# Local attention on quarter-array matmuls: 64 rows per head, unpadded keys, new priorities

## Chip, cores and metric

The kernel runs on one core of a Trainium2 chip. The metric is the device time of one execution in microseconds (us). The kernel before took 943.61 us (median of 3 runs, 941.19 to 946.57).

## What is computed

Attention of two kinds over 4 batches, 8 heads, 576 positions and 64 channels, their sum, and then two pairs of dense layers on the 2304 tokens:

```python
out_up = np.repeat(sm_attn(q_d, k_d, v_d), factor, axis=2)   # on means of 4 positions
mask = np.abs(pos[:, None] - pos[None, :]) < factor
scores = np.where(mask, scale * np.matmul(q, k.transpose(0, 1, 3, 2)), -1000000000.0)
...
out_local = np.matmul(attn, v)
x = (out_up + out_local)            # to [2304, 512]
h = x @ w_in;  y = (h * np.cos(h)) @ w_out          # first pair of layers
h = y @ w_in2; out = (np.maximum(h, 0.0) ** 2) @ w_out2   # second pair
```

## The kernel before

**Local attention** is done in units, `unit_l(b, d)`: 4 batches times 5 stretches of up to 116 queries, 20 units in all. A unit holds two blocks (`t`) of 58 queries, each against the 64 keys that can lie in its band, for 8 heads, which are held as 4 pairs (`pr`): 128 partitions hold the 64 channels of the even head of a pair and, below, those of the odd one. `f_s` makes the scores. The query tile of a pair and a block is the stationary operand (128 rows, 58 columns). The keys move, from a tile `kz` that has two copies of the columns: in one the odd head's rows are zero, in the other the even head's. So one matmul of 128 columns makes the scores of both heads, and the zeros keep them apart. Block 0 writes partitions 0 to 57 of the result, block 1 partitions 64 to 121. All 8 matmuls of a unit go into one bank of PSUM, on top of a bf16 matmul (L573) that puts the mask there. `softmax` runs on DVE and ACT, `f_t` transposes the weights on PE, `f_e` copies them on ACT into `pz`, which is zero-padded in the same way (two copies, one ACT instruction for each half of the partitions), and `f_pv` multiplies by the values, 8 matmuls again. `f_x` adds the up-sampled global part and writes the tokens to `xr`. The zeros of `kz` and `pz` are set once by POOL. `kz` and `pz` are two fixed tiles each, taken in turn; `q` and `v` have two buffers.

**Global attention** is 16 units `unit_g`. **The first pair of layers** runs in 5 rounds of 512 or 256 tokens (`mlp_h`, `mlp_o`, 16 blocks `f` each), in matmuls of fp32r; each number is split in a high and a low part, so each product is three matmuls (`mm3`, L666 to L668). Its weights are converted from float64 words on DVE (`convert`) as they arrive. A round can begin when its tokens are in `xr`. Of the 20 local units 5 come before the first round; the other 15 are put between the matmuls of rounds. **The second pair** (`big_h`, `big_o`) follows, from about 544 us on, with no attention in it.

**PSUM.** Four banks (`ps`) are shared by scores, transposes and results of the attention and by `mlp_h`; four more (`acc`) hold the sums of `mlp_o`.

**The order** on every engine is set before the run: the class `Plan` places the operations one by one, with costs and due times (`key`) that `OFF` shifts by operation and stage. Where the plan sees PE idle before the first `mlp_o`, it puts in small matmuls on zeros (`busy`, L1174), below called fills. Each engine works through its list in that order and waits on semaphores; SP issues the loads and stores in the same way. `IN_TURN` names the tiles whose buffers are given out in the order of the due times.

```python
nc.tensor.matmul(
    ps[64 * t:64 * t + QT, pr], T[q][:, t, pr, :], kz[kt][:, :, t, pr, :], start=False,
    stop=(pr == PR - 1),
)
```

Of the kernel before, what the change touches and what calls it, by code (L numbers as in the profile page):

```python
# [18 lines left out]
PR = H // 2  # L19
# [3 lines left out]
QT = 58  # L23
# [12 lines left out]
ADD_PE = 0  # L36
# [19 lines left out]
class Plan:  # L56


    RATE = {"SP": 1.24, "POOL": 2.07}
    LAT = {"PE": 0.15, "ACT": 0.15, "DVE": 0.15, "SP": 0.0, "POOL": 0.0}  # L60

    IN_TURN = ("rawi", "rawo", "w2", "p", "pt", "q", "v", "t", "w1")
# [45 lines left out]
    def order(self):  # L108
# [23 lines left out]
        stream = [x for o in sorted(ops, key=lambda o: o[2]) for x in o[5] if x[1] == "ws"]  # L132

        def room(inst, more=0):
            tag = inst[0]
            held = got[tag]
            at = len(held) + more
            if tag in self.IN_TURN and turn[tag][at] != inst:
                return None
            if inst[1] == "ws" and stream[0] != inst:  # L140
                return None
            if at < self.bufs[tag]:
                return 0.0
            last = [end[i] for i in self.users[held[at - self.bufs[tag]]]]
# [80 lines left out]
def body(ctx: ExitStack, tc: tile.TileContext, qb, kw, vw, qp, kp, vp, wi, wo, masks, ident, out_t):  # L225
    nc = tc.nc
    NR = len(ROUNDS)
    BUFS = {
        "q": 2, "v": 2, "rawi": 2, "rawo": 2, "wm": 1, "wa": 2, "w2": 3, "p": 3, "pt": 2, "t": 2, "ki": 2,
        "mx": 4, "sm": 4, "gh": 3, "gl": 3, "e": 2, "acc": 1, "ps": 4, "w1": PAIRS,  # L230
    }
    ATT = ("q", "v", "p", "pt", "mx", "sm")
# [170 lines left out]
    def load_local(b, d, key):  # L403
        q, v, kt = ("q", b, d), ("v", b, d), (b * ND + d) % 2

        def lq():
            nc.sync.dma_start(out=new(q, [128, 2, PR, QT]), in_=qb[b, d])
# [13 lines left out]
    def softmax(u, key, ps, p, view, np_, g, n, scale, on_act):  # L421
# [8 lines left out]
        def small(t):  # L430
            return T[t][0:np_, 0:g]
# [885 lines left out]
```

## Time and profile before

| | before |
|---|---|
| median of the runs, us | 943.61 (941.19 to 946.57) |
| the profiled execution, us | 936.85 |
| its span, first to last instruction, us | 935.0 |
| PE busy, us | 912.2 (98%) |
| DVE busy, us | 624.6 (67%) |
| ACT busy, us | 421.2 (45%) |
| granted clock of TensorE | 0.998 |
| first matmul of the first round, us from the start | 66.07 |

The rows name an engine, a line of kernel.py, the operation and its tiles (result, then operands). PE is the matmuls, PEld their weight loads. An fp32 matmul is two records of the profile (L579: 320 records of 160 matmuls), each with a weight load of its own. The busy time of a group is the union of its records, so records that run side by side are counted once, while the mean of one record is its length from issue to end. Idle time is charged to what ended it.

### The profile page before, as it was taken

Reading aid. Unit: us, or ns where it says so; the run is one execution under the profiler, and the core shown is the slowest. Engines: PE = TensorE matmul, PEld = TensorE weight load, DVE = VectorE, ACT = ScalarE, POOL = GpSimd, SP = SyncE. Lnnn points to the kernel's source line nnn. Section 1 sums busy time; section 2 is a strip of 40 time slices with the busy share of each in tenths; the row PEclk is TensorE's granted clock in tenths of the full one; section 3 lists DMA queues with packets and bytes.
Section 4 is the critical chain, followed back from the end, with each engine's and each line's share of the span. In section 5 each row is a group of like instructions: output and inputs, shape, how many; then the busy total and the mean of one; then the engine's idle time right before and its main releaser. Section 6 shows DMA issues by size and latency. Waiting matters only on the chain.

```text
span 935.0 us, 15239 instructions
## 1 busy us (share of the span) xinstructions
PE 912.2 (98%) x5794; PEld 793.7 (85%) x5794; DVE 624.6 (67%) x1106; ACT 421.2 (45%) x865; POOL 36.7 (4%) x53
## 2 busy tenths in 40 slices
PE   9999999999999999999999989999999999999997
PEld 9787787789788877888888879999999898999996
DVE  6898789744754269867897667878955454635351
ACT  1866568767766376656665522213221111121111
POOL 3001200220030000000000000000000000000000
PEclk9999999999999999999999999999999999999999
DMA  9876956994892255776897796878776555766543
GB/s 286 272 215 191 251 181 224 287 249 154 257 194 80 71 171 163 258 257 219 290 324 234 247 337 219 291 242 266 243 257 199 183 180 178 212 226 183 168 158 113
DMA packets 82569, 204.10 MB, mean 218 GB/s; under 512 B 9281, under 2 KB 18241, under 8 KB 82497
## 3 DMA queue, kind: packets, MB, share of 16 engines
q1 hardware_dynamic: 77888, 191.33, 62.1%
q0 software_dynamic: 4608, 11.80, 6.6%
q8 instruction: 46, 0.75, 0.3%
q14 instruction: 27, 0.21, 0.1%
HBM read 162.20 MB, written 40.89 MB: 217 GB/s over the span
## 4 chain that ended last, share of the span: by engine, by line
PE 72%; DMA 2%; ACT 1%; DVE 1%; issue 0%; SPq 0%; ACTq 0%; DVEq 0%
PE acc L666 9%; PE acc L667 9%; PE acc L668 9%; PE pp L666 6%; PE pp L667 6%; PE pp L668 6%; PE ps L666 5%; PE ps L667 5%; PE ps L668 5%; PE acx L1094 2%; PE acx L1095 2%; PE acx L1093 2%; DMA w<-w_dram 1%; PE ps L579 1%; PE ps L616 1%; PE ps L520 0%
## 5 line engine op out<-in xcount | busy, mean ns | idle before, releaser
L666 PE MATMUL ps<-xh,w 128*128 128x512 f32 (+1 forms) x320 | 120.8, 377 | 2.5 <-DVE t L706 1.9
L666 PE MATMUL acc<-gh,w 128*128 128x512 f32 (+1 forms) x320 | 120.3, 376 | 0.7 <-DMA w<-w_dram 0.7
L668 PE MATMUL acc<-gh,w 128*128 128x512 f32 (+1 forms) x320 | 118.1, 369 | 1.0 <-DVE w L276 1.0
L667 PE MATMUL ps<-xl,w 128*128 128x512 f32 (+1 forms) x320 | 118.0, 369 | 0.5 <-DVE xl L276 0.5
L668 PE MATMUL ps<-xh,w 128*128 128x512 f32 (+1 forms) x320 | 117.8, 368 | 0.0
L667 PE MATMUL acc<-gl,w 128*128 128x512 f32 (+1 forms) x320 | 117.8, 368 | 0.0
L276 DVE TENSOR_TENSOR gl<-t,gh 128x512 fp32r<-128x512 f32 (+1 forms) x80 | 50.7, 635 | 46.4 <-ACT gh L273 45.6
L706 DVE TENSOR_TENSOR t<-t,ps 128x512 f32<-128x512 f32 (+1 forms) x80 | 50.5, 632 | 39.3 <-ACT t L703 39.1
L1066 DVE TENSOR_TENSOR xl<-c,xh 128x768 fp32r<-128x768 f32 x32 | 30.6, 956 | 68.4 <-ACT xh L1063 68.2
L666 PEld LDWEIGHTS ps<-xh,w 128*128 128x128 f32 x320 | 60.2, 188 | 16.4 <-DVE t L706 3.6
L668 PEld LDWEIGHTS acc<-gh,w 128*128 128x128 f32 x320 | 60.3, 188 | 12.0 <-DVE w L276 1.8
L666 PEld LDWEIGHTS acc<-gh,w 128*128 128x128 f32 x320 | 60.3, 188 | 11.9 <-issue 1.4
L1025 DVE TENSOR_TENSOR c<-ua,pp 128x384 f32<-128x384 f32 x96 | 52.8, 552 | 24.9 <-PE pp L668 21.4
L667 PEld LDWEIGHTS ps<-xl,w 128*128 128x128 f32 x320 | 60.3, 188 | 10.2 <-DVE xl L276 0.9
L1063 ACT ACTIVATE xh<-c 128x768 fp32r<-128x768 f32 x32 | 27.0, 845 | 93.0 <-PE acc L668 84.6
L668 PEld LDWEIGHTS ps<-xh,w 128*128 128x128 f32 x320 | 60.3, 188 | 10.1
L667 PEld LDWEIGHTS acc<-gl,w 128*128 128x128 f32 x320 | 60.4, 189 | 9.4
L711 ACT ACTIVATE t<-t 128x512 f32<-128x512 f32 (+1 forms) x80 | 46.7, 585 | 47.9 <-DVE t L698 46.9
L694 ACT ACTIVATE ki<-ps 128x512 int32<-128x512 f32 (+1 forms) x80 | 43.6, 550 | 43.5 <-PE ps L668 35.8
L273 ACT ACTIVATE gh<-t 128x512 fp32r<-128x512 f32 (+1 forms) x80 | 46.6, 583 | 32.1 <-PE acc L668 27.5
L698 DVE SCALAR_TENSOR_TENSOR t<-ki,ps 128x512 f32<-128x512 int32 (+1 forms) x80 | 50.0, 629 | 7.7 <-ACT ki L694 6.9
L703 ACT ACTIVATE t<-t,halfpi 128x512 f32<-128x512 f32 (+1 forms) x80 | 54.1, 678 | 1.8
(163 smaller groups left out, 2103.2 us busy)
## 6 DMA issues: line engine op xcount, KB each, us to landing
w<-w_dram SPq DMA_DIRECT2D x96, 512.0 KB, 3.7
gl<-w_dram SPq DMA_DIRECT2D x84, 256.0 KB, 3.2
gh<-w_dram SPq DMA_DIRECT2D x84, 256.0 KB, 3.7
rawi<-in_wi_dram SPq DMA_DIRECT2D x32, 512.0 KB, 6.0
rawo<-in_wo_dram SPq DMA_DIRECT2D x32, 512.0 KB, 5.7
w_dram<-w SPq DMA_DIRECT2D x32, 512.0 KB, 4.9
w_dram<-rawo SPq DMA_DIRECT2D x24, 512.0 KB, 4.2
v<-in_vw_dram SPq DMA_DIRECT2D x20, 256.0 KB, 4.2
```

The costliest lines, as they stand in the source:

```text
L273: nc.scalar.activation(out=hi(), in_=src(), func=AF.Copy)
L276: nc.vector.tensor_tensor(out=lo(), in0=src(), in1=hi().bitcast(F32), op=OP.subtract)
L666: nc.tensor.matmul(ps, w_hi, r_hi, start=first, stop=False)
L667: nc.tensor.matmul(ps, w_hi, r_lo, start=False, stop=False)
L668: nc.tensor.matmul(ps, w_lo, r_hi, start=False, stop=last)
L694: nc.scalar.activation(out=tt(ki), in_=tt(hp), func=AF.Copy, scale=1.0 / TWO_PI)
L698: nc.vector.scalar_tensor_tensor(out=tt(t), in0=tt(ki), scalar=-TWO_PI, in1=tt(hp), op0=OP.mult, op1=OP.add)
L703: nc.scalar.activation(out=tt(t), in_=tt(t), func=AF.Sin, scale=-1.0, bias=halfpi[:, 0:1])
L706: nc.vector.tensor_tensor(out=tt(t), in0=tt(t), in1=tt(hp), op=OP.mult)
L711: "ACT", act(n), key + 0.2, lambda: nc.scalar.activation(out=tt(t), in_=tt(t), func=AF.Abs), w=[t]
L1025: nc.vector.tensor_tensor(out=out(), in0=a(), in1=ps(), op=OP.subtract if sub else OP.add)
L1066: nc.vector.tensor_tensor(out=gpart(1, R, f), in0=T[t], in1=gpart(0, R, f).bitcast(F32), op=OP.subtract)
```

## The change

- `unit_l` has no padded tiles. Keys are a tile `k` of 128 partitions, loaded by one transfer in place of two; `pz` is a tile without the second copy.
- Each score matmul works on 64 rows (one head) and writes 58 partitions: 64 columns, 16 matmuls a unit in place of 8 of 128 columns. Even heads write one bank, odd heads another. Neighbours in the list use different row halves; two heads and two blocks make four quarters of the array. The mask is added twice, 256 columns each.
- The values' product goes the same way: 16 matmuls of 58 columns on 64 rows, in two banks, in place of 8 of 116 columns on 128 rows.
- `softmax` reads the scores from two banks: maximum and subtraction are two instructions each, on half the columns. `f_x` is two instructions per piece. `f_e` is one ACT instruction of 128 partitions in place of two of 64.
- `q`, `k` and `v` have three buffers, `pz` two. POOL's memsets go.
- The plan takes the turn of buffers from the order in which operations are written; all of `OFF` is new, so all engines' lists are in a new order.

```diff
-ADD_PE = 0
...
-OFF = {('SP|body.<lambda>|wid', 0): -8.1, ('SP|body.<lambda>|wmf', 0): -24.5,
+OFF = {('SP|body.<lambda>|wid', 0): -472.0, ('SP|body.<lambda>|wmf', 0): 129.9,
...
-        for i in sorted(range(n), key=lambda i: (ops[i][2], i)):
-            for inst in ops[i][5]:
+        for o in ops:
+            for inst in o[5]:
                 turn[inst[0]].append(inst)
-        stream = [x for o in sorted(ops, key=lambda o: o[2]) for x in o[5] if x[1] == "ws"]
+        stream = [x for o in ops for x in o[5] if x[1] == "ws"]
...
-        "q": 2, "v": 2, "rawi": 2, "rawo": 2, ...
+        "q": 3, "k": 3, "v": 3, "pz": 2, "rawi": 2, "rawo": 2, ...
...
-            nc.vector.tensor_reduce(out=small(mx), in_=view(), op=OP.max, axis=AX.X)
+            nc.vector.tensor_reduce(out=small(mx)[:, i::m], in_=views[i](), op=OP.max, axis=AX.X)
...
         def f_s():
-            ps = new(s, [128, PR, 2, KT], space=PSUM)
             new(p, [128, 512])
-            nc.tensor.matmul(
-                ps.rearrange("p r h n -> p (r h) n"), id16, mask16[:, mk:mk + 1, :].to_broadcast([128, 2 * PR, KT]),
-                start=True, stop=False,
-            )
+            for x in s:
+                nc.tensor.matmul(
+                    new(x, [128, PR, KT], space=PSUM), id16, mask16[:, mk:mk + 1, :].to_broadcast([128, PR, KT]),
+                    start=True, stop=False,
+                )
             for pr in range(PR):
                 for t in range(2):
-                    nc.tensor.matmul(
-                        ps[64 * t:64 * t + QT, pr], T[q][:, t, pr, :], kz[kt][:, :, t, pr, :], start=False,
-                        stop=(pr == PR - 1),
-                    )
+                    for h in range(2):
+                        nc.tensor.matmul(
+                            T[s[h]][64 * t:64 * t + QT, pr], T[q][half[h], t, pr, :], T[k][half[h], t, pr, :], start=False,
+                            stop=(pr == PR - 1),
+                        )
...
-        def f_e(hh):
-            pp = slice(64 * hh, 64 * hh + 64)
-            nc.scalar.activation(out=pz[kt][pp, :, :, hh, :], in_=T[tp][pp, :, :, 0:QT], func=AF.Copy)
+        def f_e():
+            nc.scalar.activation(out=T[pz], in_=T[tp][:, :, :, 0:QT], func=AF.Copy)
...
                 for j in range(2):
                     for par in range(2):
-                        nc.tensor.matmul(
-                            ps[64 * par:64 * par + 64, t, 2 * j:2 * j + 2, 0:m], T[v][:, t, 2 * j + par, :],
-                            pz[kt][:, 2 * j + par, t, :, 0:m], start=not on_pe, stop=j == 1 or not on_pe,
-                        )
+                        for h in range(2):
+                            nc.tensor.matmul(
+                                T[pv[h]][half[par], t, j, 0:m], T[v][half[h], t, 2 * j + par, :],
+                                T[pz][half[h], 2 * j + par, t, 0:m], start=True, stop=True,
+                            )
```

**PE between the first and the second round.** The list of PE where the last scores before the second round stand; `acc` rows are `mlp_o` of the first round, `x4` and `x8` are counts. Before:

```order
L592 MATMUL ps<-id_sb,p 128x128 x4
L666 MATMUL acc_1456<-gh,w_2142 128x512
L667 MATMUL acc_1456<-gl,w_2142 128x512
L668 MATMUL acc_1456<-gh,w_2142 128x512
L573 LDWEIGHTS id_68
L573 MATMUL ps<-mask_69,id_68 128x512
L579 MATMUL ps<-kz_70,q 58x128 x8
L616 MATMUL ps<-pz_72,v 64x116 x8
L573 LDWEIGHTS id_68
L573 MATMUL ps<-mask_69,id_68 128x512
L579 MATMUL ps<-kz_71,q 58x128 x8
L592 MATMUL ps<-id_sb,p 128x128 x4
```

After, the same place:

```order
L574 LDWEIGHTS id_68
L574 MATMUL ps<-mask_69,id_68 128x256
L574 LDWEIGHTS id_68
L574 MATMUL ps<-mask_69,id_68 128x256
L581 MATMUL ps<-k,q 58x64 x16
L574 LDWEIGHTS id_68
L574 MATMUL ps<-mask_69,id_68 128x256
L574 LDWEIGHTS id_68
L574 MATMUL ps<-mask_69,id_68 128x256
L581 MATMUL ps<-k,q 58x64 x16
L593 MATMUL ps<-id_sb,p 128x128 x4
L611 MATMUL ps<-pz,v 64x58 x32
```

The scores of two units now stand next to each other, and no matmul of the first round's layers stands between the attention's.

**SP at the start.** The list of loads from the first on; `up_sb` and `xr` take the parts of the pooled queries and keys, `rawi` and `rawo` the weights' words. Before:

```order
L414 DMA v<-in_vw_dram 128x512 x2
L291 DMA rawi<-in_wi_dram 128x1024 x2
L291 DMA rawo<-in_wo_dram 128x1024 x2
L1178 DMA mask_f<-in_masks_dram 128x192
L1176 DMA id_sb<-in_ident_dram 128x128
L407 DMA q<-in_qb_dram 128x464 x2
L358 DMA up_sb<-in_qp_dram 128x4x144 x4
L358 DMA xr<-in_kp_dram 128x4x144 x4
L411 DMA kz_70<-in_kw_dram 64x512
```

After:

```order
L288 DMA rawi<-in_wi_dram 128x1024 x2
L1164 DMA id_sb<-in_ident_dram 128x128
L355 DMA xr<-in_kp_dram 128x4x144 x4
L355 DMA up_sb<-in_qp_dram 128x4x144 x4
L288 DMA rawo<-in_wo_dram 128x1024
L288 DMA rawi<-in_wi_dram 128x1024
L288 DMA rawo<-in_wo_dram 128x1024
L406 DMA k<-in_kw_dram 128x512 x3
L406 DMA v<-in_vw_dram 128x512 x2
```

The pooled queries and keys moved ahead of the values, the mask, the local queries and the second matrix's weights. On PE the plan puts 180 small matmuls ahead of the first one of the attention, where 350 stood, and 645 in all ahead of the first round, where 646 stood.

**DVE in the units between the first and the second round.** `mx` is the maximum, L440 and L431 the subtraction, `sm` the sums. Before:

```order
L437 TENSOR_REDUCE mx<-ps 128x8
L440 TENSOR_TENSOR p<-ps,mx 128x512
L459 TENSOR_REDUCE sm<-p 128x8
L437 TENSOR_REDUCE mx<-ps 128x8
L463 TENSOR_SCALAR sm<-sm 128x8
```

After:

```order
L428 TENSOR_REDUCE mx<-ps 128x4 x2
L431 TENSOR_TENSOR p<-ps,mx 128x4x64 x2
L451 TENSOR_REDUCE sm<-p 128x8
L428 TENSOR_REDUCE mx<-ps 128x4
L455 TENSOR_SCALAR sm<-sm 128x8
```

The rows that read PSUM became two each, one for each bank.

## Rows read from the trace of the kernel before

**Rows 1.** The page: busy time, share of the span and instructions of each engine.

```profile
PE 912.2 (98%) x5794; PEld 793.7 (85%) x5794; DVE 624.6 (67%) x1106; ACT 421.2 (45%) x865; POOL 36.7 (4%) x53
```

**Rows 2.** Busy time by stretch: length; PE, PEld, DVE, ACT, POOL; clock, DMA share, GB/s.

```profile
0.00:20.00 20.00, 19.01 (x293) 19.01 (x294) 12.55 (x28) 3.81 (x5) 6.33 (x13) 1.00 0.93 283
...
40.00:140.00 100.00, 96.41 (x693) 79.45 (x692) 83.79 (x150) 65.53 (x151) 9.75 (x13) 1.00 0.72 211
140.00:300.00 160.00, 153.34 (x1179) 129.47 (x1178) 104.77 (x224) 115.27 (x283) 19.76 (x26) 1.00 0.77 211
300.00:440.00 140.00, 140.00 (x775) 113.00 (x774) 93.00 (x171) 82.91 (x151) 0.00 (x0) 1.00 0.53 181
440.00:560.00 120.00, 115.67 (x524) 96.09 (x523) 93.96 (x159) 66.44 (x113) 0.00 (x0) 1.00 0.82 286
```

**Rows 3.** Waits of PE and PEld: total us, times, longest.

```profile
PE ps L666 <- DVE t L706: 1.9, 4, 0.7
...
PEld ps L666 <- DVE t L706: 3.6, 8, 0.9
```

**Rows 4.** Group of the scores' matmuls: count, busy us, mean ns, idle before.

```profile
L579 PE MATMUL ps<-kz,q 128*58 128x128 f32 x320 | 21.8, 278 | 0.3 <-DMA kz<-in_kw_dram 0.2
```

**Rows 5.** Timeline of PE, a stretch of two units: start, length, count.

```profile
354.37 1.01 PE L616 MATMUL ps<-pz,v 128*64 128x116 f32 x16
355.32 0.39 PE L573 MATMUL ps<-mask,id 128*128 128x512 bf16 x1
355.64 1.09 PE L579 MATMUL ps<-kz,q 128*58 128x128 f32 x16
356.66 0.39 PE L573 MATMUL ps<-mask,id 128*128 128x512 bf16 x1
```

**Rows 6.** The same L579 group, records begun by 355.79, by 355.81, by 355.91.

```profile
355.64 0.32 PE L579 MATMUL ps<-kz,q 128*58 128x128 f32 x2
355.64 0.43 PE L579 MATMUL ps<-kz,q 128*58 128x128 f32 x4
355.64 0.54 PE L579 MATMUL ps<-kz,q 128*58 128x128 f32 x6
```

**Rows 7.** Timeline of PE before the first round (L1174 fills, L504 global scores).

```profile
0.99 22.36 PE L1174 MATMUL idle<-zero 128*128 128x128 bf16 x350 [0.99 <-DVE zero L1168]
24.13 1.88 PE L504 MATMUL ps<-kd_sb,qd_sb 128*96 128x144 f32 x12 [0.78 <-DVE kd_sb L368]
...
60.49 2.84 PE L1174 MATMUL idle<-zero 128*128 128x128 bf16 x48
...
66.07 0.48 PE L666 MATMUL ps<-xh,w 128*128 128x512 f32 x1
```

**Rows 8.** DVE before the first round: the first conversion, and mean ns by form.

```profile
8.23 0.43 DVE L295 TENSOR_SCALAR wm<-rawi 128x512 int32<-128x512 int32 x1 [6.08 <-DMA rawi<-in_wi_dram]
...
L302 DVE SCALAR_TENSOR_TENSOR wa<-rawi,wm 128x512 int32<-128x512 int32 x16 | 11.0, 690 | 0.4
...
L368 DVE TENSOR_TENSOR kd_sb<-kd_sb,xr 128x144 f32<-128x144 f32 x8 | 2.5, 308 | 0.3
```

**Rows 9.** Groups of the units' DVE and ACT work: count, busy us, mean ns.

```profile
L437 DVE TENSOR_REDUCE mx<-ps 128x8 f32<-128x512 f32 x20 | 13.7, 685 | 7.0 <-PE ps L579 6.9
...
L440 DVE TENSOR_TENSOR p<-ps,mx 128x512 f32<-128x512 f32 x16 | 10.8, 672 | 0.2
...
L642 DVE TENSOR_TENSOR xr<-ps,up_sb 128x464 f32<-128x464 f32 x13 | 8.2, 632 | 1.3 <-PE ps L616 1.3
...
L642 DVE TENSOR_TENSOR xr<-ps,up_sb 128x232 f32<-128x232 f32 x7 | 2.8, 395 | 1.2 <-PE ps L616 1.2
...
L596 ACT ACTIVATE pz<-ps 64x464 f32<-64x464 f32 x40 | 22.0, 551 | 7.3 <-PE ps L592 6.9
```

**Rows 10.** Busy time in one stretch between the first rounds (columns as rows 2).

```profile
175.00:180.00 5.00, 4.38 (x49) 3.40 (x45) 4.69 (x12) 3.50 (x9) 1.41 (x3) 1.00 1.03 347
```

**Rows 11.** L573 (the masks) from 300 to 440 us: count, durations, first and last start.

```profile
L573 PE MATMUL ps<-mask,id x5: 381/389/390, 344.5 to 356.7; 128*128 128x512 bf16 x5
```

More of the change, by code (lines that the diff above doesn't have):

```diff
@@ L475, in f_norm @@
             )
-        op("DVE", dve(g * n), key, f_max, r=[ps], w=[mx], new=[mx])
+        for i in range(m):
+            op(
+                "DVE", dve(g * n // m), key, lambda i=i: f_max(i), r=[ps[i]] + ([mx] if i else []), w=[("mx1",) + u] if i else [mx],
+                new=[] if i else [mx],
+            )
         if on_act:
-            op("ACT", g * act(n, 0.18) + 0.2, key + 0.02, f_exp_sum, r=[ps], w=[p, sm, mx], new=[sm], table="exp")
+            op("ACT", g * act(n, 0.18) + 0.2, key + 0.02, f_exp_sum, r=list(ps) + [("mx1",) + u] * (m - 1), w=[p, sm, mx], new=[sm], table="exp")
         else:
-            op("DVE", dve(g * n), key + 0.01, f_sub, r=[ps, mx], w=[p])
-            op("ACT", act(g * n), key + 0.02, f_exp, w=[p], table="exp")
+            for i in range(m):
+                op(
+                    "DVE", dve(g * n // m), key + 0.01, lambda i=i: f_sub(i), r=[ps[i], mx] + [("mx1",) + u] * (m - 1),
+                    w=[("p1",) + u] if i else [p],
+                )
+            op("ACT", act(g * n), key + 0.02, f_exp, r=[("p1",) + u] * (m - 1), w=[p], table="exp")
             op("DVE", dve(g * n), key + 0.03, f_sum, r=[p], w=[sm], new=[sm])
@@ L565, in unit_l @@
         u = ("l", b, d)
-        s, p, tp = ("ps", "s") + u, ("p",) + u, ("ps", "t") + u
-        q, v, kt = ("q", b, d), ("v", b, d), (b * ND + d) % 2
+        s, tp, pv = [("ps", "s", h) + u for h in range(2)], ("ps", "t") + u, [("ps", "pv", h) + u for h in range(2)]
+        p, q, k, v, pz = ("p",) + u, ("q", b, d), ("k", b, d), ("v", b, d), ("pz",) + u
         mk = {0: 0, ND - 1: 2}.get(d, 1)
+        half = [slice(0, 64), slice(64, 128)]
         def f_s():
-            ps = new(s, [128, PR, 2, KT], space=PSUM)
@@ L598, in unit_l @@
-        op("PE", 0.5, key + 0.1, f_t, r=[p, ("id",)], w=[tp], new=[tp])
-        for hh in range(2):
-            op("ACT", act(464), key + 0.1, lambda hh=hh: f_e(hh), r=[tp], w=[("pz", kt, hh)])
+        def f_e():
+            nc.scalar.activation(out=T[pz], in_=T[tp][:, :, :, 0:QT], func=AF.Copy)
+        op("PE", 0.6, key + 0.1, f_t, r=[p, ("id",)], w=[tp, pz], new=[tp, pz])
+        op("ACT", act(464), key + 0.1, f_e, r=[tp], w=[pz])
         s0 = DT * d
         n = min(DT, S - s0)
-        on_pe = b * ND + d < ADD_PE
@@ L604, in unit_l @@
-        pv = ("ps", "pv") + u
         def f_pv():
-            ps = new(pv, [128, 2, KD, QT], space=PSUM)
+            for x in pv:
+                new(x, [128, 2, 2, QT], space=PSUM)
             for t in range(2):
                 m = min(QT, n - t * QT)
-                if on_pe:
-                    nc.tensor.matmul(
-                        ps[:, t, :, 0:m], id_sb, up_sb[:, :, s0 + t * QT:s0 + t * QT + m], start=True, stop=False
-                    )
                 for j in range(2):
@@ L624, in unit_l @@
+        op(
+            "PE", 0.6, key + 0.2, f_pv, r=[v, pz] + [("up", c) for c in range(KD)], w=pv + xtok(b * S + s0, n), new=pv,
         )
```

93 lines of the change are left out of this document (36 added, 57 removed).

## Prediction, made before the changed kernel ran

> **What bounds the kernel now.** I read the page's busy times first. PE has work for 98% of the span, and DVE, the next, for 67% [rows 1]. Then the stretches: from 40 to 560 us PE stands idle for 3.6, 6.7, 0 and 4.3 us, about 14.6 us in all [rows 2]. So a microsecond that PE no longer needs between the rounds is worth up to a microsecond, unless another engine is right behind. The granted clock is full in every stretch [rows 2], so nothing is to be won or lost there unless PE falls idle for long. Third I looked at what PE waits for: the largest item between the rounds is the next block's scores bank, which L706 on DVE still reads, 1.9 and 3.6 us [rows 3]. The four `ps` banks are thus already a resource that PE waits for, though little. PE never waits for the units' keys for more than 0.3 us in all [rows 4], so third buffers have nothing to remove on PE. Last comes the time before the first round, which begins at 66.07 us [rows 7]. There the plan fills PE with matmuls on zeros, so a busy PE says nothing of the bound, and 350 fills alone take the first 23 us.
>
> **Part 1, the matmuls.** A unit's scores take from 355.64 to 356.66, 1.02 us, and its values' product from 354.37 to 355.32, 0.95 us [rows 5]. Each has 16 records. One record is listed at 278 ns [rows 4], so they overlap, and rows 6 show how: two records have begun by 355.79, four by 355.81, six by 355.91. They start in pairs, about 107 ns apart after the first step. That is what 2 x 128 columns take at 2.4 GHz (256 / 2.4 = 107 ns). So each record streams its columns twice, and the two blocks, which write different halves of the result's partitions, run side by side. The pairs could not form if a matmul's second record had to start ahead of the next matmul's first; records of different tiles pass each other. The scores are then 8 steps x 107 = 0.85 us and 0.17 us fixed (the first weights, the drain). The product is 8 x 2 x 116 / 2.4 = 0.77 us and 0.18 us fixed.
>
> Now there are 32 records of half the columns. If four run side by side (two blocks times two heads), it is 8 steps again, each 2 x 64 / 2.4 = 53 ns for the scores and 48 for the product. The first step of a group is 0.05 us longer than the others (355.64 to 355.80, against 0.107 us) [rows 6], which I take as the load of the first weights, so a step won't be shorter than about 55 ns. Scores 8 x 55 + 170 = 0.61 us (0.41 saved), product 8 x 55 + 180 = 0.62 us (0.33 saved). The mask is one matmul of 512 columns and 0.32 us from its start to the next one's [rows 5]; two of 256 have the same columns, 0.01 us more. **0.73 us a unit; 15 units between the rounds: -10.9 us.** No row shows 64-row halves side by side, so the bounds are wide. If the two halves don't overlap, it is 16 steps of 53 and 48 ns, 0.85 and 0.77 us: nothing saved. If not even the pairs formed, 32 steps would be 1.70 and 1.55 us, 1.6 us dearer a unit; the pairs in rows 6 speak against that. I take the first, since blocks already run side by side by the place they write to.
>
> One rule speaks against it. The rows show two records that begin less than 20 ns after each other and the next two some 100 ns later [rows 6]. The Trainium skill, "TensorE: Matmul & The Clock Gate", section "Wait — 56ns, not 53.3ns?", says that matmuls never start closer than about 25 ns, however few columns they have. By it four records would need an estimated 100 ns, as long as a pair does now, and the saving would be gone. The rows don't agree with it for neighbours in a pair.
>
> **Part 2, what it adds elsewhere.** DVE reads two banks: an addition of 464 columns takes 632 ns and one of 232 takes 395 [rows 9], so a split costs 2 x 395 - 632 = 0.16 us. Maximum, subtraction and addition are split: 0.48 us a unit, 9 us of DVE for 20 units. Over the whole run DVE has room; between the first rounds it has not: 4.69 of 5 us at 175 us, where PE has 4.38 [rows 10]. There the chain of a unit (scores, maximum, subtraction, exponential, sum, norm, transpose, product) sets when the next round may start, and two of the splits lie on it. ACT gives one copy of 551 ns back on that chain [rows 9]. PE's list there is also tighter: scores of two units next to each other take all four banks, and no matmul of the layers stands between them. I charge one split, 0.16 us, for each of 15 units: **+2.4 us**. Bounds: -4 us (the new list closes a quarter of PE's 14.6 us idle) to +8 us (idle grows by half).
>
> Loads, buffers and memsets: the same bytes in fewer transfers, and nobody on PE waits for them [rows 4]; POOL is 4% busy [rows 1]. Zero, covered by PE's own work; without that cover it could only be the 0.3 us that PE waits for keys.
>
> **Part 3, before the first round.** The plan kept 645 of 646 fills, so what PE is given is shorter only by the units' saving, 5 x 0.73 = 3.7 us. But 180 fills stand ahead of the first global scores, where 350 did. 350 take until 23.4 us; a fill is about 57 ns in a later run (48 from 60.49 to the next row's start, or 2.84 us less the last one's drain) [rows 7], so 180 end near 13.7 us. DVE must by then have done two conversions, the four sums of keys and one of queries. The first weights land at 8.23 us now [rows 8]; 512 KB of values go ahead of them, some 1.8 us at the 283 GB/s of the first 20 us [rows 2], so about 6.4 us after. Two conversions are eight instructions of up to 0.69 us, about 5.0 us; four sums of keys are 12 x 0.31 us, one of queries 4 x 0.31 us [rows 8], 5.0 us. The scores start at 16.4 us, and PE waits 2.7 us where it waits 0.78 [rows 7]. A late start isn't made up, since the fills behind it run in any case: 1.9 us lost. **-3.7 + 1.9 = -1.8 us**, bounds -3.7 (not late) and +1.9 (no saving on PE).
>
> **Sum.** -10.9 + 2.4 - 1.8 = -10.3 us. The terms are from an execution of 936.85 us (span 935.0, 1.85 us around it), which gives 926.5; it lies 0.7% under the median, 943.61, to which the runs after compare. **943.6 - 10.3 = 933.3 us.**
>
> **Rivals.**
> - *Two at a time.* The halves of 64 rows take turns. Nothing is saved (16 steps of half the columns), the splits and the late start stay: 943.6 + 2.4 + 1.9 = 948, or 944 where the list hides both; I take 946. For it: no row shows row halves. Against: rows 6.
> - *Given back.* Four run side by side, but before the earlier rounds DVE is the bound, and PE idles for what it saves in 10 units; only the last five, at 344 to 357 us [rows 11], in a stretch without PE idle [rows 2], and the head gain: -5 x 0.73 - 1.8 = -5.5, about 938. For it: rows 10. Against: DVE has 105 us of work in the 160 us from 140 us on [rows 2].
> - *The banks, slower than before.* A unit holds two of the four `ps` banks from its scores until its last subtraction: two maxima and two subtractions, 4 x 0.42 = 1.7 us, at least. If the next matmul on PE, another unit's transpose or the next block of the layers, needs a third and fourth bank and waits this out at each of 15 units, it costs 25 us less the 10.9 and 1.8: +12, about 956. It decides from 12.7 / 15 = 0.85 us of waiting a unit. For it: the pair of scores without layers between, and PE's waits for L706 [rows 3]. Against: these are 5.5 us now, and `acc` matmuls need no `ps` bank.
>
> **How the numbers follow.** My forecast has 0.58 (923 to 940 with the bounds of part 2 and the head), two at a time 0.15, given back 0.12, the banks 0.15. The range 923 to 948 holds the forecast but for a few hundredths, given back and two at a time: 0.81. About 0.5% (4.7 us: 938.9 to 948.3) is what a measurement can tell from no change. Faster: nearly all of the forecast's 0.58 and half of given back, 0.62. Slower: the banks and a part of two at a time, 0.17. Same: 0.21.
>
> **What would show it.** Right: scores of a unit in about 0.6 us from first to last record, eight records begun within two steps where four are; the first global scores near 16 us, with a wait of 2 to 3 us ahead; the first round near 64 us; PE idle in 40 to 560 us not above 17 us. Two at a time: scores still near 1.0 us. Given back: short scores, but PE idle of 20 us or more between 140 and 300 us. The banks: PE's waits for `ps` tiles, by DVE's maxima and subtractions, at the top of its list. I would be wrong in kind if the second pair of layers, from 560 us on, changed by more than 2 us, since only its order is new there.

## The result and the profile after

The changed kernel takes **955.46 us** (median of 4 runs, 950.13 to 956.17), beside 942.40 us for the kernel before on the same chip (4 runs): 1.0117 times, 95% interval 1.0073 to 1.0161. It is slower, by about 11 to 13 us; the prediction had it 10 us faster. The profiled execution took 956.17 us, span 954.1.

The page's line of engines, which answers to [rows 1]: PE's busy time is unchanged (912.2 before), so the saving isn't visible there, and PE stands idle 18 us more.

```profile
PE 913.1 (96%) x6461; PEld 794.7 (83%) x6461; DVE 629.6 (66%) x1172; ACT 416.5 (44%) x849; POOL 32.8 (3%) x47
```

Busy time by stretch, as [rows 2] (length; PE, PEld, DVE, ACT, POOL; clock, DMA share, GB/s):

```profile
0.00:20.00 20.00, 16.99 (x203) 16.49 (x204) 14.60 (x40) 4.61 (x13) 2.58 (x7) 0.92 0.98 300
20.00:40.00 20.00, 14.13 (x130) 12.07 (x129) 10.83 (x25) 10.53 (x37) 0.83 (x1) 0.67 0.72 237
40.00:140.00 100.00, 96.93 (x1028) 81.24 (x1027) 82.43 (x159) 59.13 (x152) 9.84 (x13) 1.00 0.71 206
140.00:300.00 160.00, 145.38 (x1447) 123.63 (x1446) 107.78 (x256) 102.82 (x247) 19.59 (x26) 0.96 0.75 213
300.00:440.00 140.00, 140.00 (x926) 113.08 (x925) 89.67 (x179) 88.49 (x167) 0.00 (x0) 1.00 0.50 170
440.00:560.00 120.00, 120.00 (x593) 99.37 (x592) 91.58 (x163) 71.42 (x121) 0.00 (x0) 1.00 0.75 260
```

Two things are new. The granted clock, full everywhere in the first profile of before (0.83 from 20 to 40 us in its second one, e17), is 0.67 from 20 to 40 us and 0.96 from 140 to 300. And in that last stretch PE is idle for 160 - 145.38 = 14.6 us, where it was 6.7. PE's waits over the run (total us, times, longest), where [rows 3] stood at the top between the rounds:

```profile
PE ps L538 <- DMA vd_sb<-in_vp_dram: 5.9, 1, 5.9
PE acx L1081 <- DMA w<-w_dram: 5.4, 7, 1.2
...
PE ps L593 <- DVE p L431: 2.4, 2, 1.4
...
PE ps L538 <- ACT pt L523: 2.2, 1, 2.2
PE ps L504 <- DVE qd_sb L376: 2.0, 2, 1.1
PE ps L593 <- ACT xh L270: 1.5, 1, 1.5
PE ps L593 <- DVE xr L631: 1.3, 1, 1.3
```

The matmuls themselves did what was forecast. The timeline of PE up to three moments after the start of a unit's scores, which answers to [rows 5, 6]: four records have begun by 46.70, eight by 46.79, and all 32 are followed by the next mask 0.61 us after the first began (1.02 before).

```profile
46.66 0.28 PE L581 MATMUL ps<-k,q 64*58 64x64 f32 x4
...
46.66 0.34 PE L581 MATMUL ps<-k,q 64*58 64x64 f32 x8
...
46.66 0.67 PE L581 MATMUL ps<-k,q 64*58 64x64 f32 x32
47.27 0.39 PE L574 MATMUL ps<-mask,id 128*128 128x256 bf16 x2
```

The head is where most is lost. PE's timeline there, as [rows 7]:

```profile
15.01 0.98 PE L504 MATMUL ps<-kd_sb,qd_sb 128*96 128x144 f32 x6 [1.10 <-DVE qd_sb L376]
...
24.00 0.66 PE L520 MATMUL ps<-id_sb,p 96*72 96x96 f32 x6
30.53 1.23 PE L538 MATMUL ps<-pt,vd_sb 72*64 72x144 f32 x8 [5.87 <-DMA vd_sb<-in_vp_dram]
31.69 1.46 PE L1162 MATMUL idle<-zero 128*128 128x128 bf16 x12
```

The pooled values `vd_sb` are summed by four transfers, each behind the last. Before, L538 asked for them at 33 us. Now it asks at 24.66, they are whole at 30.5, and PE stands for 5.87 us. Behind the wait twelve fills take 1.46 us from the first to the last one's end; at full clock, in e5, the same twelve take 0.84. The first round begins at 76.63 us instead of 66.07.

**One profile is not enough.** Two more profiles were taken of the unchanged kernels (e17 and e18, below). With them, in us, from PE's first matmul of the first round and of the second pair, and the last instruction:

| profile | first round begins | from there to the second pair | from there to the end |
|---|---|---|---|
| before / again (e17) | 66.07 / 69.30 | 476.78 / 478.10 | 392.19 / 394.27 |
| after / again (e18) | 76.63 / 77.44 | 480.42 / 479.27 | 397.04 / 393.98 |
| mean difference | +9.4 | +2.4 | +2.3 |

The sum, 14.0, is near the 11 to 13 of the medians. So: **the head lost 9, the stretch with the units didn't gain its 8.5 but lost 2, and the second pair, which was to be neutral, lost about 2.** The last two are as small as what two profiles of one kernel differ by, 1 to 3 us in these columns.

### The profile page after: what moved, and what is told of

Its sections match the earlier page's. It is cut to its first block, busy times and chain, and to the rows that moved or that the text cites. A ratio compares the mean times of both kernels' runs of the same rounds, so it can differ in the third digit from the quotient of the medians.

```text
span 954.1 us, 16668 instructions
## 1 busy us (share of the span) xinstructions
PE 913.1 (96%) x6461; PEld 794.7 (83%) x6461; DVE 629.6 (66%) x1172; ACT 416.5 (44%) x849; POOL 32.8 (3%) x47
## 4 chain that ended last, share of the span: by engine, by line
PE 70%; DMA 12%; issue 9%; DVE 5%; ACT 4%; POOL 0%; SPq 0%; ACTq 0%; POOLq 0%; DVEq 0%
PE acc L654 10%; PE acc L655 10%; PE acc L656 10%; PE pp L654 5%; PE pp L656 5%; PE pp L655 5%; PE ps L654 5%; PE ps L655 5%; PE ps L656 5%; DMA w<-w_dram 5%; DMA qn_sb<-in_qp_dram 3%; PE acx L1081 2%; DMA vd_sb<-in_vp_dram 2%; PE acx L1083 2%; PE acx L1082 2%
## 5 line engine op out<-in xcount | busy, mean ns | idle before, releaser
L654 PE MATMUL ps<-xh,w 128*128 128x512 f32 (+1 forms) x320 | 122.1, 381 | 1.5 <-DVE t L694 1.1
L656 PE MATMUL ps<-xh,w 128*128 128x512 f32 (+1 forms) x320 | 119.5, 373 | 0.0
L654 PEld LDWEIGHTS acc<-gh,w 128*128 128x128 f32 x320 | 60.5, 189 | 15.5 <-ACT t L699 2.0
L654 PEld LDWEIGHTS ps<-xh,w 128*128 128x128 f32 x320 | 61.7, 193 | 14.1 <-DVE t L694 3.0
L656 PEld LDWEIGHTS ps<-xh,w 128*128 128x128 f32 x320 | 61.7, 193 | 10.3
L1020 ACT ACTIVATE ua<-pp 128x384 f32<-128x384 f32 x24 | 11.7, 489 | 110.5 <-PE pp L656 108.9
L1013 DVE TENSOR_TENSOR ua<-ua,pp 128x384 f32<-128x384 f32 x72 | 39.8, 553 | 29.1 <-PE pp L656 26.0
```

The costliest lines, as they stand in the source:

```text
L654: nc.tensor.matmul(ps, w_hi, r_hi, start=first, stop=False)
L656: nc.tensor.matmul(ps, w_lo, r_hi, start=False, stop=last)
L1013: nc.vector.tensor_tensor(out=out(), in0=a(), in1=ps(), op=OP.subtract if sub else OP.add)
```

## The experiments

Each ran on a chip beside the kernel before, whose median was 941 to 943.6 us throughout. "Stretch" is from the first round to the second pair. `OFF` is the table of order numbers.

**e17 and e18, the same kernels again** (no edit).

> The kernel before, unchanged, for a second profiled execution. In e16, whose head has the list of the kernel before, PE waited 4.9 us for the keys' sums and the first round began at 69.7 us, against 0.78 and 66.07 in the first profile. Theory (the time at which the pooled keys land differs by some microseconds from execution to execution, and the first profile was a lucky one, as its 936.9 us against a median of 942 to 943 says): the first round begins at 67 to 70 us with a wait of 2 to 5 us; the rest of the span, from the first round to the end, is within 2 us of the first profile's 869.0. Rival (e16's late head comes from its own edit): 66 us and a wait under 1.5 us again.

> The changed kernel, unchanged, for a second profiled execution and more runs. Theory (the wait for the pooled values and the half clock behind it belong to the list): the first round begins at 74 to 78 us, from there to the end it takes within 2 us of the first profile's 877.5, and the median is 953 to 956. Rival (the first profile's head was an unlucky one): the first round begins before 72 us, and the median is 950 or less.

Medians 942.0 (10 runs) and 952.96 (4 runs), ratio after to before 1.0131 (1.0103 to 1.0158). PE's waits ahead of the first round, of before and then of after:

```profile
PE ps L504 <- DVE kd_sb L368: 3.5, 1, 3.5
```

```profile
PE ps L538 <- DMA vd_sb<-in_vp_dram: 5.4, 1, 5.4
```

The first profile of before was a lucky one (0.78 us of wait for the keys' sums), and its head varies by 3 us. The late head of after doesn't go away. The rest of after's span was 873.3 us, not within 2 us of 877.5, and that of before 872.4, not within 2 us of 869.0: these parts of both theories fell, and with them most of what the second pair seemed to lose.

**e2, three of four parts of the first block's pooled values left out.** The sum is then not the pooled values; everything else is unchanged.

```diff
+ def f_in(dst, src, r, how):
+     if b or r == 0:
+         nc.gpsimd.dma_start(out=dst, in_=src[b, r], accum_op=how)
...
```

> The changed kernel, but of the four transfers that sum the pooled values of the first batch only the first is issued; the other three are left out, all lists else are the same. Theory A, the late pooled values make PE wait at 24 us and the clock falls behind that wait: no such wait, full clock from 24 to 41 us, the first round at 66 to 68 us in place of 76.6, 945 to 948 us in all. Theory B, the head is late for DVE and the loads of keys and queries: the first round at 74 us or later.

941.96 us (one run). First round at 65.79, no wait for `vd_sb`; the clock from 20 to 40 us:

```profile
20.00:40.00 20.00, 19.20 (x330) 16.66 (x328) 14.85 (x32) 13.08 (x53) 0.00 (x0) 1.00 0.75 255
```

That is the whole loss of the head, but with 864 KB less to move in a stretch whose DMA share is 0.98, so it doesn't separate the wait from the traffic.

**e10 and e13, the fills.** e10 adds fills where PE stands idle; every semaphore wait stays in the program. e13 adds the same and takes as many out behind.

```diff
+ ahead = {("f_s", "s", "g", 0, 0): 18, ("f_s", "s", "g", 0, 1): 15, ("f_pv", "pv", "g", 0, 0): 100}
+ keep = {91: 0, 48: 27}   # e13 only: length of a group of fills, and how many of it stay
...
```

> The changed kernel with 133 more matmuls on zeros in the head: 18 and 15 ahead of the first two global scores and 100 ahead of the first global product, where PE stands idle for 1.1, 0.9 and 5.9 us. All waits stay. Theory (of the head's 10.6 us some 5 are the half clock behind the wait for the pooled values): the granted clock is full from 20 to 60 us, the first round begins 4 to 5.5 us earlier, near 71.5 us, and the time falls by as much. Rival (the clock costs nothing by itself, PE would wait for DVE and ACT there): the first round stays within 1.5 us of 76.6.

950.53 us (1.0081, 1.0048 to 1.0114). The clock is full and the first round begins at 72.99, 3.6 us earlier than in the first profile of after and 4.5 earlier than in the second:

```profile
20.00:40.00 20.00, 18.08 (x279) 16.48 (x277) 13.03 (x28) 11.12 (x38) 0.82 (x1) 1.00 0.76 252
```

> The changed kernel with as many matmuls on zeros in the head as it has, but 133 of them moved: 18 and 15 stand ahead of the first two global scores and 100 ahead of the first global product, and as many are taken out behind it (all 91 ahead of the first local scores, 21 each of the next two groups of 48). No other row of PE moves and no other engine's list changes. Theory (the head was lost because PE asks for the pooled values 6 us early and then still runs its fills at half clock): PE fills the wait with work it has to run in any case, the first round begins at 66 to 68 us instead of 76.6, and the time falls by 9 to 11 us, to about 945. Rival (what is late at the start stays late, since DVE's and ACT's first sums and conversions end the head): the first round stays at 71 us or later, the time at 950 or above.

946.49 us (1.0047, 1.0027 to 1.0068): 6 to 9 us less by moving 133 matmuls on zeros. The first round begins at 71.22, which is the rival's figure (71 or later), while the time is nearer the theory's 945 than the rival's 950. The values land as late as ever (L538 starts at 31.76), but now a new wait shows, PE's first local mask, which DVE converts:

```profile
PE ps L574 <- DVE mask L1171: 2.6, 1, 2.6
```

**e5, e6 and e12, the values sooner.** In e5 parts 2 and 3 go to free tiles and GpSimd adds them; e6 also has the second pair's `OFF` of before; e12 is e7 (below) with VectorE adding and 33 fills more.

```diff
+ if b or r < 2:
+     nc.gpsimd.dma_start(out=dst, in_=src[b, r], accum_op=how)
...
+ nc.gpsimd.tensor_tensor(out=dst[:, i], in0=dst[:, i], in1=y, op=OP.add)   # e12: nc.vector
...
```

> The changed kernel, but two of the four parts of the first block's pooled values no longer wait for the part before: they go into tiles that are free at the start, and GpSimd adds them to the sum. The list of PE is the same. Theory (the values that land near 30 us, and the half clock behind that wait, make the loss of the head and some of the loss between the rounds): the values are whole near 22 us, PE doesn't wait 5.9 us at L538, the first round begins near 66 us, and the time falls by 12 to 14 us, to about 942. Rival (the head is late because the transfers of the first 20 us crowd each other, whatever their order): the extra transfers at 9 us push the keys' sums back, PE waits ahead of the first global scores instead, the first round stays behind 72 us and the time above 950.

948.01 us (1.0066, 1.0043 to 1.009), first round at 71.73. The wait for the values is gone, and one of 5.9 us for the sums of queries has come. DVE's timeline, then GpSimd's:

```profile
13.81 0.65 DVE L372 TENSOR_TENSOR up_sb<-up_sb 128x144 f32<-128x144 f32 x2
...
17.47 1.99 DVE L372 TENSOR_TENSOR up_sb<-up_sb 128x144 f32<-128x144 f32 x2 [2.36 <-DMA up_sb<-in_qp_dram]
19.49 2.54 DVE L376 TENSOR_TENSOR qd_sb<-up_sb 64x144 f32<-64x144 f32 x2
```

```profile
16.75 2.54 POOL L405 TENSOR_TENSOR vd_sb<-vd_sb,vd_e 72x512 f32<-72x512 f32 x2 [5.80 <-DMA vd_e<-in_vp_dram]
19.26 2.60 POOL L405 TENSOR_TENSOR vd_sb<-vd_sb,vd_ki 72x512 f32<-72x512 f32 x2
```

This wait was 0.9 us in the changed kernel. Of what it grew by, some 2 us are the queries' part, which lands at 17.4 us instead of 15.5, and some 3 us are DVE's additions, three to four times as long while GpSimd adds.

> As e5, and the order numbers of the second pair of layers are those of the kernel before. Theory (the waits for weights in the second pair come from its new list, independent of the head): another 5.5 to 7 us, about 936, with the stretch from the second pair's first matmul to the end near 391.5 us. Rival (they come from how the work behind the head is shifted in time): the stretch is 395 us or more, and the time stays near 941.

946.44 us (1.0047, 1.0022 to 1.0072). The part from the second pair on took 392.93 us: neither the theory's 391.5 nor the rival's 395 or more, and only 1.8 less than in e5.

> As e7, with two more changes in the head: VectorE instead of GpSimd adds the two late parts of the pooled values (four instructions, about 2.5 us, behind the first normalization), and 33 more matmuls on zeros stand ahead of the first two global scores. Theory (in e5 to e7 GpSimd's additions from 16.75 to 21.9 us slowed VectorE's sums of queries, 1.74 and 2.53 us for two where two take 0.64 and 0.62, and that is where PE's new wait of 5 to 6 us came from): the sums are back at 0.65 us for two, the wait falls under 2.5 us, the first round begins at 66 to 68 us, and the time falls by 3 to 4 us, to about 941, level with the kernel before. Rival (the queries' parts land late because of the earlier transfers of values, whoever adds): the wait stays at 4 us or more and the first round behind 70 us.

948.7 us (1.0051, 1.0031 to 1.0072). DVE's sums are back at 0.65 us for two, so GpSimd was the cause of their length; but a part of the queries now lands at 19.5 us, and the profiled head ended at 77.02 (this execution, 952.14 us, was the slowest of e12's twelve). The rival holds for the rest: with the values brought forward (e5 to e8, e11, e12) the third of the queries' four parts lands at 17.9 to 20.1 us, and at 16.4 and 16.5 in the changed kernel. In the first 20 us, where the DMA share is 0.97 or more in e5, e6, e7 and e12, to bring one transfer forward was to put another back.

**e9, the head's old order.** `OFF` of before for head and second pair, fills cut to before's 350 and 296, and the fills of e7.

> The changed kernel with the order numbers of the kernel before for the head and for the second pair of layers, the fills of the head cut to 350 ahead of the first global scores and 296 behind them (as in the kernel before), and the 112 matmuls on zeros of e7 between the rounds; the pooled values come as in the changed kernel. Theory (the head was lost by asking for the pooled keys and values 9 us before they land; with the old order the units' saving of 5 x 0.7 us shows): the values are there when L538 asks near 33 us, the first round begins near 63 us, and the time is about 937, 0.5% under before. Rival (the new transfers, or the four banks, cost the head its saving in any order): the first round begins at 66 us or later, and the time stays at 941 or above.

947.18 us (1.0045, 1.0022 to 1.0067). First round at 69.15, as before's second profile (69.30): PE waits 3.0 us for the keys' sums, as it does there. With that order nothing is lost in the head, and the five units' 3.7 us of part 3 don't show there either. The 0.45% that remain are thus not the head's, and with the second pair's old list and e7's fills they lie mainly between the rounds: the stretch is 480.86 us in its one profile, against 476.78 and 478.10.

**e3, the second pair's old order** (`OFF` of the last stage is before's).

> The changed kernel with the priorities of the kernel before for the second pair of layers alone (stage 4). Theory A, its new list issues the loads of the second matrix too late: PE's waits for w in the second pair go (5.4 us now), the stretch from the first product to the end is 392 us in place of 397, 950 to 951 us in all. Theory B, these waits come from the first layers' late end or from a busier memory: 397 us as now.

948.17 us (one run); 391.30 us from the second pair on, without the waits for `w` at L1081. Over all profiles with the new list that part took 392.5 to 397.0 us (7 profiles, mean 394.4), over all of the new kernel with the old list there and the new one between the rounds 391.3 to 393.2 (9, mean 392.4; e1, with the old list everywhere, 396.6): the new list costs 2 us, not the 6 of a single pair of profiles. The kernel before took 392.2, 394.3 and 392.9 us for it (its two profiles and e16), so against before it is hardly more than 1 us.

**e7, the clock between the rounds.** 112 matmuls on zeros at six places where PE stood; they add nothing to a result.

```diff
+ plug = {("f_pv", "pv", "g", 1, 0): (34, ("acc", 0, 0, 0)),
+     ("f_t", "t", "l", 1, 1): (18, None), ("f_t", "t", "l", 1, 2): (18, None), ("f_h", "h", 0, 1, 0): (6, None),
+     ("f_t", "t", "l", 2, 2): (14, None), ("f_t", "t", "l", 2, 3): (22, None)}
...
```

The place in the changed kernel, PE's timeline from one unit's product into the second round:

```profile
183.10 0.69 PE L611 MATMUL ps<-pz,v 64*64 64x58 f32 x32
185.12 0.63 PE L593 MATMUL ps<-id_sb,p 128*128 128x128 f32 x4 [1.33 <-DVE xr L631]
...
189.37 0.63 PE L593 MATMUL ps<-id_sb,p 128*128 128x128 f32 x4 [1.37 <-DVE p L431]
...
193.84 0.41 PE L656 MATMUL ps<-xh,w 128*128 128x256 f32 x1
194.05 0.41 PE L654 MATMUL ps<-xh,w 128*128 128x256 f32 x1
```

Layers' matmuls of 256 columns start 213 ns apart here, and 120 ns apart from 198 us on: the first is the lower of the two levels, 1.2 GHz, behind the gaps.

> As e6, with 112 matmuls on zeros put into PE's list at six places between the rounds where PE stands idle for 0.4 to 2.2 us (34 ahead of the first global product of the second block, 42 behind the first round, 36 behind the second); they add nothing to any result. Theory (the clock falls to half behind these gaps and PE pays for it in what follows, about 1.3, 3.6 and 1.8 us): the granted clock stays full from 140 to 300 us, and the time falls by 4 to 7 us, to about 930. Rival (the gaps are waits for DVE and ACT, and the half clock lies under the same waits): within 1.5 us of e6.

The clock holds where the fills stand (in the changed kernel 0.91, 0.83 and 0.91 in these windows):

```profile
160.00:180.00 20.00, 19.68 (x250) 14.96 (x249) 16.37 (x43) 14.41 (x43) 0.00 (x0) 1.00 0.83 274
180.00:200.00 20.00, 17.55 (x257) 15.80 (x256) 14.94 (x45) 12.17 (x32) 7.20 (x10) 1.00 0.96 239
260.00:280.00 20.00, 17.91 (x178) 13.71 (x178) 13.53 (x32) 12.25 (x21) 7.01 (x8) 1.00 1.02 239
```

But 945.05 us (1.0031, 1.0007 to 1.0054) is 1.4 us under e6: the rival. What the full clock saves is mostly waited out elsewhere; where, this run doesn't show.

**e14, all three together** (e13, e3 and e7).

> As e13, with the second pair's order numbers of the kernel before (as e3) and the 112 matmuls on zeros between the rounds (as e7). Theory (the three losses, head, second pair and half clock between the rounds, are separate and add up): another 5.5 and 2 to 5 us less, about 936, 0.7% under the kernel before. Rival (a gain in one place is a longer wait in the next, for DVE's chain and for the weights' transfers): not under 941.

945.42 us (1.0015, 0.9998 to 1.0031): level with the kernel before, the best of those that compute the same thing, and no gain. The rival again. What its stretch is made of, worked out by giving each PE matmul the time from its start to the next one's and adding these up by kind, in us:

| from the first round to the second pair | before (e17) | after (e18) | e14 |
|---|---|---|---|
| scores, product, masks of local units | 35.29 | 30.69 | 24.60 |
| the other attention matmuls | 31.76 | 34.31 | 32.30 |
| layers, 512 columns | 357.58 | 360.11 | 357.89 |
| layers, 256 columns | 52.36 | 53.14 | 53.20 |
| matmuls on zeros | 1.11 | 1.01 | 8.94 |
| sum | 478.10 | 479.27 | 476.94 |

With the clock kept the units' matmuls are 10.7 us shorter, and 7.8 us of fills stand where PE would otherwise wait. The time is free, and nothing fills it. In e18 the units' row is 6.1 us longer than in e14: waits and half clock behind these matmuls.

The row of the other attention matmuls has a wait of its own. The pooled keys of the third batch come by a chain of four transfers too. They land at 219.2 us in the first profile of after, where PE asks at 220.3; in e18 PE waits 2.3 us for them, in e14 2.5. This wait, of 1.1 to 4.4 us, stands in 10 of the 16 profiles with the new list between the rounds, and in none of the three with the list of before (its two profiles and e16).

**e4 and e8, what the shorter matmuls are worth.** The loop over the two halves goes outermost, so that the halves are no neighbours in PE's list (e4 on the changed kernel, e8 on e7). In the product, whose loop over the two blocks stays outside (not shown), they are then four matmuls apart.

```diff
-for pr in range(PR):
-    for t in range(2):
-        for h in range(2):
+for h in range(2):
+    for pr in range(PR):
+        for t in range(2):
...
```

> The changed kernel, but the loop over the two heads of a pair is outermost in the scores and in the product, so neighbours in the list use two quarters of the array, not four. Theory A, four records overlap because four neighbours use four quarters: scores take 1.0 us a unit in place of 0.61, product 0.95 in place of 0.62, 11 to 15 us more in all, 966 to 970. Theory B, the queue looks past 16 records and finds the other half anyway: 0.6 us and 955 us.

957.4 us (one run), 2 to 4 us over the changed kernel's medians, where 11 to 15 were expected. A unit's scores then take 0.87 us, between the two expectations, and the product 0.66 where it took 0.62:

```profile
47.53 0.94 PE L581 MATMUL ps<-k,q 64*58 64x64 f32 x32
48.40 0.39 PE L574 MATMUL ps<-mask,id 128*128 128x256 bf16 x2
...
58.83 0.73 PE L611 MATMUL ps<-pz,v 64*64 64x58 f32 x32 [0.61 <-ACT pz L596]
59.49 0.66 PE L593 MATMUL ps<-id_sb,p 128*128 128x128 f32 x4
```

> As e7, with the heads' halves no longer neighbours in PE's list: all 16 matmuls of one half, then all 16 of the other, in scores and product, so a unit takes about 0.45 us longer on PE. It tells whether PE's own time between the rounds reaches the end once the clock holds. If PE is the bound there: 15 units times 0.45 us, about 7 us slower than e7. If DVE and ACT are: at most 2 us slower.

948.25 us, 1.0067 (1.0041 to 1.0093) against e7's 1.0031: 3.4 us for an expected 7. But the units didn't become 0.45 us longer. Scores and product last as long as in e4, 0.3 us more a unit, which is some 4.6 us for 15 units. Most of what PE needs longer here reaches the end; the two intervals leave room for nothing of it and for all.

**e11, e15 and e16, DVE.** Maxima and sums of the local units read every second key (so the softmax is another one): 0.53 us a unit less on the chain. e11 on e6, e15 on e14, e16 on the kernel before.

```diff
-            nc.vector.tensor_reduce(out=small(mx)[:, i::m], in_=views[i](), op=OP.max, axis=AX.X)
+            x = views[i]()
+            nc.vector.tensor_reduce(out=small(mx)[:, i::m], in_=x[:, :, ::2] if n == KT else x, op=OP.max, axis=AX.X)
...
```

> As e6, with less for DVE in each local unit: the maxima read every second key and the sums the first half of the keys, so the softmax is another one; about 0.17 us less for each of two maxima and 0.3 us less for the sum, all on the chain from a unit's scores to its product. PE's list is unchanged. Theory (between the rounds the chain over DVE sets when PE may go on, so what PE saved there turned into waits): the stretch from the first round to the second pair falls by 5 to 9 us from 483.5 us, and the time by as much. Rival (the stretch is set by PE itself, by the weights' transfers or by ACT): it falls by less than 2 us.

943.17 us, 1.0008 (0.9988 to 1.0029) against e6's 1.0047; stretch 477.28 against 483.50. These two profiles differ in one thing more, PE's wait for the third batch's pooled keys, in e6 and then in e11:

```profile
PE ps L519 <- DMA kd_sb<-in_kp_dram: 4.4, 1, 4.4
```

```profile
PE ps L521 <- DMA kd_sb<-in_kp_dram: 1.1, 1, 1.1
```

With the waits for weights, 4.0 of the 6.2 us are shorter waits for transfers. Those that DVE ended come to 6.0 us in both.

> As e14, with DVE's work cut in each local unit as in e11 (maxima and sums read every second key, so the softmax is another one; by the durations in e11 2 x 0.13 + 0.27 = 0.53 us a unit). Theory (what PE saved on the scores and products is eaten by the chain over DVE, in repaired lists too): the stretch from the first round to the second pair falls from 476.9 us to 470 to 473, the time to about 940. Rival (with the clock kept, PE and the weights' transfers set the stretch): it falls by under 2 us.

941.8 us, 0.9998 (0.9979 to 1.0018) against e14's 1.0015; its stretch, 477.65, didn't fall. The experiment was badly built: the fills stand in PE's list and take their 8 us whatever DVE does.

> The kernel before with the same cut of DVE's work (its maxima and sums read every second key, so the softmax is another one; about 0.54 us a unit). Theory (before, PE was the bound between the rounds and DVE's chain had a little room; the shorter matmuls used it up): the stretch from the first round to the second pair falls by under 3 us from 476.8, the time by under 4 us. Rival (DVE's chain held PE up before the change as much as after it): it falls by 5 us or more, as in e11.

942.52 us, 1.0001 (0.9982 to 1.002): no gain. By the medians the same DVE work is worth 0.39% (0.1 to 0.7 by the two intervals) in the changed kernel's list without fills, and nothing in the kernel before. That is a sign that DVE's chain holds PE up between the rounds now and didn't before, by 3.7 us of the 8 that were taken away. It is no proof: in the profiles the waits that DVE ended didn't fall, and those for transfers did.

**e1, the new matmuls in the old order** (`OFF` of before, its names mapped to the new operations).

> The changed kernel with the priorities of the kernel before (an entry whose operation was split goes to both halves; the turn of buffers stays new). Theory A, the matmuls save what was worked out and the new lists lose it: first round at 62 to 66 us, scores 0.61 us a unit, the second pair of layers 392 us long as before, about 929 us in all. Theory B, two banks and the split reads cost the time in any order: PE idles 14 us or more between the first and the last round again, 945 us or more.

971.8 us (1.0315, 1.0279 to 1.0351); the stretch is 505.6 us, and PE stands idle for 31 us of it, 24 of them until DVE is done. These are theory B's figures, but they don't decide for it, since the list is neither the old nor the new one: the plan put 757 fills ahead of the first round where before has 646. The likely reason, not tried, is that the old numbers only shift what the plan chooses between, and with other costs it chooses otherwise. What the matmuls are worth without a new order between the rounds was therefore not measured.

## Why the prediction was wrong

**The price of the matmuls: right.** Eight steps of about 55 ns were forecast, scores 0.61 us and product 0.62. Eight records had begun within two steps; scores took 0.61 us, the steps are 56 ns, and 15 units are 10.7 us shorter in e14 where 10.9 was forecast. The rule weighed there, that matmuls never start closer than 25 ns (the Trainium skill, "TensorE: Matmul & The Clock Gate", section "Wait — 56ns, not 53.3ns?"), doesn't hold for the four quarters: within a step the records start 7 ns apart. The same page's section "The mechanism" has about 4 ns for tiles of a pack, which is nearer.

**The splits: right in size.** DVE's groups, as [rows 9]:

```profile
L428 DVE TENSOR_REDUCE mx<-ps 128x4 f32<-128x256 f32 x40 | 15.7, 414 | 7.6 <-PE ps L581 7.5
...
L431 DVE TENSOR_TENSOR p<-ps,mx 128x256 f32<-128x256 f32 x32 | 12.3, 416 | 0.1
L631 DVE TENSOR_TENSOR xr<-ps,up_sb 128x232 f32<-128x232 f32 x26 | 9.6, 386 | 0.4 <-PE ps L611 0.2
```

A split maximum costs 2 x 414 - 685 = 143 ns, near the 0.16 us forecast.

**That the saving lies on the path: wrong.** This is the first step that failed: "-10.9 us" was put on PE's path for 15 units, with 2.4 us taken off. With the clock kept the matmuls are shorter by that much (e14), but the stretch isn't (479 to 480 us against 477 to 478): PE's idle from 140 to 300 us went from 6.7 to 14.6 us, that of 40 to 560 us to 17.7 (not above 17 was the sign of being right), and part of the rest ran at half clock. That is near the rival "given back", dismissed because DVE has 105 us of work in 160 us [rows 2], but its sign, 20 us of idle or more, wasn't reached, and its cause, DVE, isn't shown. Added up by what ended them, PE's waits in the stretch are, in the two profiles of after against the two of before: for DVE 6.7 and 5.5 us against 5.2 and 6.4, for ACT 5.6 and 5.4 against 2.2 and 2.3, for transfers 2.6 and 3.4 against 1.0 and 0. So what grew, beside the half clock, are the waits for ACT and for transfers; whether ACT was late for DVE's sake wasn't followed. The mean over 160 us was the wrong view in any case: in the five units ahead of each round a step waits for the one before it, and [rows 10] had DVE at 4.69 of 5 us there. Which chain holds PE stays open; ACT, the weights and the third batch's keys were not tried alone.

**The head: wrong by 11 us.** The forecast took -3.7 + 1.9 and checked only the first matmul that was brought forward, the global scores. Those came out near it (start 15.0 us, waits of 1.1 and 0.9, where 16.4 and 2.7 were forecast). The step that failed is "Loads, buffers and memsets [...] Zero": 170 fewer fills ahead bring forward every operation behind them, and L538 asks for values that arrive by a chain of four transfers, each some 7 us, whose last landing, at 31.7 us in the trace of before, was to be read there. The second half is that "the fills behind it run in any case": they did, at half clock. e10 prices that at 3.6 us or a little more, and e13 the order of the fills as a whole at 6 to 9.

**The second pair: nearly right.** It was to be neutral within 2 us, and the new list costs 1 to 2 (e3 and the nine profiles, and those of before).

**The banks,** the rival that gave 956, came near the time by another way: PE's waits for DVE's subtractions and additions are 3.7 us between the rounds, not 25.

**The base.** All terms were made against one profile whose head was 3 us better than the next one's. That moved no sign here, but the difference of two single profiles (19 us) overstated the loss by half. The bounds, too, don't add up as written: -10.9 - 4 - 3.7 and -10.9 + 8 + 1.9 give 925 to 942.6 us, not 923 to 940. The measured time lies outside either.

## What to carry to other kernels

When an order moves work forward, list every operand of everything behind that point and read when each lands, above all those that arrive by a chain of transfers; put work that has to run in any case (fills, other stages) into the wait, not behind it: here that gave 6 to 9 us back and kept the clock full up to 40 us (e13). A saving on the busiest engine need not reach the end, even at 98% busy: look for what else closes within the same few units, in windows of a few microseconds and not by a mean over the stage. And profile the unchanged kernel twice before subtracting stages of single profiles.

## What was unexpected of the hardware

Four matmuls on quarters of the array start 7 ns apart and step every 56 ns, and the order in the list matters for it: the same 32 records of the scores with the halves apart took 0.87 us instead of 0.61 (e4), while the product, with its halves only four matmuls apart, lost 0.04. While GpSimd adds in SBUF, DVE's additions of two SBUF operands take three to four times as long, 1.99 and 2.54 us for two instead of 0.65 and 0.62 (e5), and 0.65 again once DVE adds by itself (e12). The Trainium skill, "SBUF — State Buffer", section "Who interferes with whom", says that a DVE instruction with two SBUF inputs contends with a GpSimd instruction that reads SBUF; the trace agrees.
